# A scan and a gated MLP on one core: new orders for five queues, tiles assigned by a table, and PSUM banks in two sets

## The chip, the cores and the metric

The kernel runs on one core of one Trainium2 chip. The metric is the device time of one execution in microseconds (us), the median of several runs. The kernel before was timed three times: 179.22, 179.46 and 179.83 us. Lower is better.

The engines are named as in the profile: PE multiplies matrices, ACT evaluates functions and copies, DVE works on vectors, POOL does a few small things, SP starts nearly all DMA transfers. Each of them takes its instructions strictly in the order in which they were emitted.

## The reference

For x of shape 2048 x 512 (bfloat16), xn is x with each row normalized. Two branches read xn, and their product is added to x:

```python
xn = _layernorm(x, axis=-1)
Bu = einsum(xn, B_bar)                 # complex, 512 states; B_bar = (exp(dt*Lam)-1)/Lam * B
for t in range(2048): h = Lam_bar * h + Bu[t]
s = 2 * einsum(hseq, C).real + xn * Dskip
g = silu((gelu(xn @ w_gate) * (xn @ w_up)) @ w_down)    # 512 -> 1376 -> 512
out = x + s * g
```

## The kernel before

The 2048 rows are cut into four slabs of 512 (s = 0 to 3), and each slab into four tiles of 128 rows (m = 0 to 3). The steps of a slab are these; the line numbers are those of the profile.

* **Normalizing.** Slab 0 is centred tile by tile as its rows land (`center`, L341 to L350), turned by PE through PSUM (`head_t`, L315, L330, copied by L321, L323, L332 into `xcT`) and scaled only when products leave PSUM. Slabs 1 to 3 are normalized on ACT into the one buffer `xna` (L756); slab 1 takes its sums on DVE (L281), slabs 2 and 3 take theirs on ACT (L751). Each slab's `xna` is then turned by one DMA (`dma_t4`, L362) into `xnT`.
* **Gated products.** For each tile PE multiplies by `w_up` and `w_gate`, in column pieces of 512, 512 and 352 (L384, L402 for slab 0; L434 for the others). ACT takes each piece out of PSUM, plainly or through gelu (L392, L408, L437). DVE multiplies the two (L416, L418, L443, L445) into `at`, and a DMA turns `at` into `atT` (`at_t`, L450).
* **Down products.** Eleven matmuls a tile with `w_down` (`down_pair`, L466), then silu on ACT into `g2` (L469). Gelu and silu lie in different function tables of ACT, so a change from one to the other costs a table load.
* **The scan.** In two halves of 256 states (`half`), PE multiplies xn by B (L529), ACT copies to `U` (L531), DVE rotates (L541, then L549 or L553 into `W`), scans along time (L560, four a half), carries the last state on (L570 to L573) and rotates back (L541, then L549 or L553 into `hst`).
* **The output.** For each tile ACT writes `sk` = xn x Dskip into a PSUM bank (L478), PE adds eight matmuls of `hst` with the scaled C (`y_part`, L482), DVE multiplies by `g2` (L487) and adds x (L492), and a DMA writes the rows (L495). The last tile is done in two halves of 256 columns.

Setting up, DVE builds rotation tables (L621, copied by ACT at L628 and L629) and the scaled C (L724, L727, from `tF` that ACT writes at L722). C is loaded turned by DMA (L720) into the place of the second `hst`.

The order of the work is written out by hand: each call adds a numbered step to a `Plan`, and `ORDER` (L21 to L45) is the list of step numbers in which the steps are emitted. It mixes the queues of all engines; within each engine it fixes the sequence. The planned durations in the calls are not used when the kernel is built. Two of the eight PSUM banks (`ybank`) hold output tiles, and six (`ring`) are handed out in turn by `bank()` in the order of the calls. Buffers of `at`, `gt`, `ub`, `U`, `g2`, `yg`, `ot` and `sk` follow from the tile's number.

In the order before, PE does slab 0's gated products, slab 0's eight scan products (L529), then slab 0's four down products (L466), and only then slab 1's first products. SP starts, after the last weight of the gates: x of slab 1, Dskip's row, B's imaginary part, `xnT` of slab 0, B's real part, `wd`, three `atT`, x of slab 2, the fourth `atT`, `xnT` of slab 1.

Of the kernel before, what the change touches and what calls it, by code (L numbers as in the profile page):

```python
# [44 lines left out]
)  # L45


class Plan:

    def __init__(self):
        self.steps = []
        self.wrote = {}
        self.read = {}

    def add(self, eng, cost, emit, reads=(), writes=(), **planned):
# [9 lines left out]
        self.steps.append((emit, deps - {n}))  # L67
        return n

    def run(self):  # L70
        done = set()
        for i in ORDER:
            emit, deps = self.steps[i]
            assert deps <= done
            emit()
            done.add(i)
        assert len(done) == len(self.steps)
# [3 lines left out]
def kernel(  # L81
# [63 lines left out]
    gt = [sb(f"gt{i}", [P, F]) for i in range(NGT)]  # L145
    ub = [sb(f"ub{i}", [P, F]) for i in range(NGT)]
# [9 lines left out]
    sk = [sb(f"sk{i}", [P, M, D]) for i in range(2)]  # L156
    NG2 = 3
    g2 = [sb(f"g2_{i}", [P, 2, D], FP32) for i in range(NG2)]
# [9 lines left out]
    NR = 6  # L168
    ring = [psum.tile([P, D], FP32, name=f"ring{i}") for i in range(NR)]
    ybank = [psum.tile([P, D], FP32, name=f"ybank{i}") for i in range(2)]  # L170
# [4 lines left out]
    pl = Plan()  # L175
    DV, AC = 0.075, 0.075
# [46 lines left out]
    W1, W2 = CH[0][1], CH[1][1]  # L223
# [54 lines left out]
    def stats(m):  # L278
        r = 250.0 - 20 * m if m < M else 0.0
        order = head if m == 0 else []  # L280
        dve(512, lambda: V.bn_stats(out=st[:, m, :], in_=x_tok[:, m, :]), [("x", m // M, m % M)], [("st", m)], rank=r, after=order)  # L281
# [13 lines left out]
    def dummies(k, i):  # L295
        def f():
            for j in range(k):
                T.matmul(ybank[j][:] if j < 2 else ring[i][:], lhsT=warm[:, 0:P], rhs=warm, start=True, stop=True)  # L298
        pl.add(PE, k * 0.427, f, [], [("bank", i), ("y", 0), ("y", 1)], lag=0.22, not_before=0.6)

    def fill(k, i):
        def f():
            for _ in range(k):
                T.matmul(ring[i][:], lhsT=warm[:, 0:P], rhs=warm, start=True, stop=True)
        pe(k, 512, f, [], [("bank", i)])

    def head_t(m):

        if m == 0:
            for i in range(2):  # L310
                tp = ring[4 + i][:].bitcast(BF16)[:, 0 : D // 2].rearrange("p (k t) -> p k t", t=P)
# [4 lines left out]
                pe(2, P, f, [("xc", 0, i), "ident"], [("bank", 4 + i)])  # L316
            for i in range(2):
                tp = ring[4 + i][:].bitcast(BF16)[:, 0 : D // 2].rearrange("p (k t) -> p k t", t=P)
                dst = xcT[:, 2 * i : 2 * i + 2, 0:P]
                if i == 0:  # L320
                    head.append(dve(256, lambda tp=tp, dst=dst: V.tensor_copy(out=dst, in_=tp), [("bank", 4)], [("xcT", 0, 0)], rate=2.0, rank=500.0, after=head[-1:]))  # L321
                else:
                    acts(256, lambda tp=tp, dst=dst: act(out=dst, in_=tp, func=AF.Copy), [("bank", 5)], [("xcT", 0, 1)], rank=500.0)  # L323
            return
        bank, key = ybank[(m + 1) % 2], ("y", (m + 1) % 2)
        tp = bank[:].bitcast(BF16)[:, 0:D].rearrange("p (k t) -> p k t", t=P)
# [7 lines left out]
    head, sums0 = [], []  # L334

    def center(m):

        x = x_tok[:, m, :]
        if m == 0:
# [3 lines left out]
            dve(c, lambda: V.tensor_scalar(out=yg[0][:, 0:c], in0=x[:, 0:c], scalar1=1.0 / D, scalar2=None, op0=ALU.mult, op1=ALU.add,  # L343
                                           accum_out=ma[:, 0:1]), [("x", 0, 0)], [("yg", 0, 0), ("ma", 0)], base=0.15, rank=400.0, after=early)
            head.append(dve(512, lambda: V.tensor_scalar(out=xn[0], in0=x, scalar1=ma[:, 0:1], scalar2=mb[:, 0:1], op0=ALU.subtract, op1=ALU.subtract),
                            [("x", 0, 0), ("ma", 0), "mb"], [("xc", 0, 0), ("xc", 0, 1)], rate=2.3, rank=400.0, after=head[-1:]))
# [18 lines left out]

    def skip(s, m):
        dve(512, lambda: V.tensor_tensor(out=sk[s % 2][:, m, :], in0=xn[m], in1=Drow[:], op=ALU.mult),
            [("xn", m), "Drow"], [("sk", s % 2, m)], rate=2.0)


    ring_n = [0]

    def bank():
        r = ring_n[0] % NR
        ring_n[0] += 1
# [457 lines left out]
```

## Time and profile before

| | |
|---|---|
| timed runs | 179.22, 179.46, 179.83 us (median 179.46) |
| profiled execution | span 178.6 us from first to last instruction; its own time is not listed apart from the timed runs, which lie 0.6 to 1.2 us above the span |
| PE | busy 173.1 us (97%), 849 matmuls |
| DVE | busy 156.2 us (87%), 252 instructions |
| ACT | busy 125.1 us (70%), 240 instructions, nine of them table loads of 1.28 us |
| DMA | 18.66 MB moved; busy in nearly every slice up to 45 us, then in bursts |
| granted PE clock | 1.000 |

The span counts from the first to the last instruction. A group's row gives its line, engine, operation and tiles, then the busy time in all, the mean of one instruction in ns, and the idle time of the engine just before such an instruction with what ended it. Instructions of one engine overlap a little, so two starts lie closer together than one duration. A matmul row's mean is longer than the step from one matmul to the next, since matmuls are pipelined: four matmuls of 512 columns take 0.86 us in the chain of waits, and four of 352 columns 0.60 us.

### The profile page before, as it was taken

To read this page: it belongs to the slowest core of one execution; us is meant where nothing else is said; L and a number is where in the kernel's file an instruction comes from. 1 tells how busy PE (TensorE), PEld (TensorE's weight loads), DVE (VectorE), ACT (ScalarE), POOL (GpSimd) and SP (SyncE) were. 2 spreads that over 40 slices of the span, in tenths; PEclk is the share of its full clock that TensorE was granted. 3 is DMA by queue.
4 is the path that set the end of the run, shared out by engine and by line. 5 is a ranking of instruction groups with operands and counts; after the bars stand their busy time and mean duration, and the time that the engine had idled before them with its cause. 6 is when DMAs were issued, how large, how long until landed. Compare 5 with 4: busy or idle time off the path is not lost.

```text
span 178.6 us, 2422 instructions
## 1 busy us (share of the span) xinstructions
PE 173.1 (97%) x849; PEld 82.6 (46%) x849; DVE 156.2 (87%) x252; ACT 125.1 (70%) x240; POOL 10.2 (6%) x25
## 2 busy tenths in 40 slices
PE   8999999699999999999999999999999999999992
PEld 2545554244445554444445544444444455454451
DVE  2859997999769986999999979999999899999664
ACT  6879999969899998996619965474353872474510
POOL 2660020000100000000002000000000000000000
PEclk9999999999999999999999999999999999999999
DMA  5999999999700008920500007529300021077012
GB/s 153 266 343 276 151 275 162 215 278 224 141 0 0 0 0 154 179 60 0 110 0 31 4 2 146 111 68 157 79 25 4 0 51 33 29 161 171 0 37 81
DMA packets 47939, 18.66 MB, mean 104 GB/s; under 512 B 40280, under 2 KB 47288, under 8 KB 47928
## 3 DMA queue, kind: packets, MB, share of 16 engines
q1 hardware_dynamic: 47904, 18.52, 49.4%
q8 instruction: 6, 0.10, 0.2%
q14 instruction: 5, 0.04, 0.1%
q10 hardware_dynamic: 24, 0.00, 0.0%
HBM read 6.46 MB, written 2.10 MB: 48 GB/s over the span
## 4 chain that ended last, share of the span: by engine, by line
PE 87%; DMA 5%; DVE 3%; ACT 3%; issue 0%
PE ring L434 31%; PE ring L466 21%; PE ybank L482 15%; PE ring L529 12%; DMA atT<-at 5%; PE ring L384 3%; PE ring L402 1%; ACT gt L408 1%; PE ring L298 1%; DVE st L281 1%; PE ybank L384 1%; ACT at L392 1%; DVE yg L487 1%; DVE at L416 1%; ACT L408 1%; DVE ot L492 1%
## 5 line engine op out<-in xcount | busy, mean ns | idle before, releaser
L434 PEld LDWEIGHTS <-xnT 128*128 128x128 bf16 x288 | 28.2, 98 | 28.4
L466 PE MATMUL ring<-wd,atT 128*128 128x512 bf16 (+1 forms) x176 | 39.2, 379 | 1.5 <-DMA atT<-at 1.5
L434 PE MATMUL ring<-wu,xnT 128*128 128x512 bf16 (+1 forms) x144 | 32.3, 357 | 0.0
L434 PE MATMUL ring<-wg,xnT 128*128 128x512 bf16 (+1 forms) x144 | 32.1, 357 | 0.0
L560 DVE TENSOR_TENSOR_SCAN Fs<-rho,ini,W 128x512 bf16<-128x512 f32 x24 | 29.6, 1271 | 0.1
L529 PE MATMUL ring<-xnT,BT 128*128 128x512 bf16 x128 | 29.3, 379 | 0.0
L482 PE MATMUL ybank<-C,hst 128*128 128x512 bf16 x120 | 27.9, 379 | 0.0
L466 PEld LDWEIGHTS <-atT 128*128 128x128 bf16 (+1 forms) x176 | 17.1, 98 | 22.6 <-DMA atT<-at 1.9
L437 ACT ACTIVATE ub<-ring 128x512 bf16<-128x512 f32 (+1 forms) x36 | 19.1, 557 | 11.2 <-PE ring L434 10.8
L437 ACT ACTIVATE gt<-ring 128x512 bf16<-128x512 f32 (+1 forms) x36 | 19.1, 559 | 7.7 <-PE ring L434 7.6
L531 ACT ACTIVATE U<-ring 128x512 bf16<-128x512 f32 x32 | 18.0, 599 | 4.2 <-PE ring L529 4.1
L541 DVE TENSOR_TENSOR Q<-U,tab 128x4096 bf16<-128x4096 bf16 x8 | 18.3, 2291 | 1.8 <-ACT U L531 1.1
L482 PEld LDWEIGHTS <-hst 128*128 128x128 bf16 x136 | 13.3, 98 | 13.9
L529 PEld LDWEIGHTS <-BT 128*128 128x128 bf16 x128 | 12.5, 98 | 15.0
L469 ACT ACTIVATE g<-ring 128x512 f32<-128x512 f32 x16 | 9.3, 595 | 14.2 <-PE ring L466 14.2
L541 DVE TENSOR_TENSOR Q<-Fs,tab 128x4096 bf16<-128x4096 bf16 x8 | 18.3, 2290 | 0.2
L487 DVE TENSOR_TENSOR yg<-ybank,g 128x512 bf16<-128x512 f32 x15 | 10.2, 687 | 6.6 <-PE ybank L482 6.6
L478 ACT ACTIVATE ybank<-sk 128x512 f32<-128x512 bf16 x15 | 9.1, 609 | 3.8 <-DVE yg L487 3.8
L751 ACT ACTIVATE junk<-x_tok 128x512 bf16<-128x512 bf16 x16 | 10.1, 642 | 1.7 <-DMA x_tok<-in_A_x_dram 1.7
L402 PE MATMUL ring<-wg,W 128*128 128x512 bf16 (+1 forms) x48 | 9.5, 357 | 0.0
L756 ACT ACTIVATE xna<-x_tok,nb,rs 128x512 bf16<-128x512 bf16 x12 | 9.4, 822 | 0.0
L560 DVE TENSOR_TENSOR_SCAN Fs<-rho,W 128x512 bf16<-128x512 f32 x8 | 9.3, 1208 | 0.0
(124 smaller groups left out, 169.8 us busy)
## 6 DMA issues: line engine op xcount, KB each, us to landing
out_dram<-ot SPq DMA_DIRECT2D x15, 128.0 KB, 1.7
x_tok<-in_A_x_dram SPq DMA_DIRECT2D x3, 512.0 KB, 5.1
wg<-in_B_w_gate_dram SPq DMA_DIRECT2D x1, 1376.0 KB
wd<-in_B_w_down_dram SPq DMA_DIRECT2D x1, 1280.0 KB
wu<-in_B_w_up_dram SPq DMA_DIRECT2D x6, 128.0 KB, 2.4
x_tok<-in_A_x_dram SPq DMA_DIRECT2D x4, 128.0 KB, 2.2
wu<-in_B_w_up_dram SPq DMA_DIRECT2D x1, 352.0 KB, 4.6
wu<-in_B_w_up_dram SPq DMA_DIRECT2D x1, 256.0 KB
```

What stands on the lines that cost most here:

```text
L402: T.matmul(ps[:, 0 : b - a], lhsT=xcT[:, k, m * P : (m + 1) * P], rhs=wt[:, k, a:b], start=(k == 0), stop=(k == KT - 1))
L434: T.matmul(ps[:, 0 : b - a], lhsT=xnT[:, s % 2, m, k, :], rhs=wt[:, k, a:b], start=(k == 0), stop=(k == KT - 1))
L437: acts(b - a, lambda: act(out=dst[:, a:b], in_=ps[:, 0 : b - a], func=AF.Copy if up else AF.Gelu_apprx_tanh), [("bank", r)], [key], table= ...
L466: T.matmul(ps[:], lhsT=atT[:fs, k, m * P : (m + 1) * P], rhs=wd[:fs, k, :], start=(k == 0), stop=(k == NFT - 1))
L482: T.matmul(ps, lhsT=hst[s % 2][:, j // NPT, j % NPT, m * P : (m + 1) * P], rhs=C2[:, j // NPT, j % NPT, c0:c1], start=(j == 0 and not seed ...
L487: dve(w, lambda: V.tensor_tensor(out=yg[e][:, c0:c1], in0=ps, in1=g2[gi][:, b, c0:c1], op=ALU.mult), [key, ("g2", gi, b)], [("yg", e, c0)])
L529: T.matmul(ps[:], lhsT=BT[:, ri, k, pt * P : (pt + 1) * P], rhs=xnT[:, s % 2, :, k, :], start=(k == 0), stop=(k == KT - 1))
L531: acts(512, lambda q=q, ri=ri, ps=ps: act(out=U[ui][:, ri, q, :], in_=ps[:], func=AF.Copy), [("bank", r)], [("U", ui, q, ri)])
L541: dve(4096, lambda: V.tensor_tensor(out=Qf, in0=src.unsqueeze(1).to_broadcast(WQ), in1=table, op=ALU.mult), reads, ["Q"], rate=2.0)
L560: pl.add(DVE, 1.12 if s == 0 else 1.185, lambda ri=ri, q=q, pt=pt, first=first: V.tensor_tensor_scan(out=Fs[:, ri, q, :], data0=rho[:, pt ...
L751: acts(512, lambda i=i, fn=fn, sc=sc, m=m: act(out=junk()[:], in_=x_tok[:, s * M + m, :], func=fn, scale=sc, accum_out=sx[:, s, i, m : m + ...
L756: acts(512, lambda m=m: act(out=xn[m], in_=x_tok[:, s * M + m, :], func=AF.Identity, scale=rs[:, s, m : m + 1], bias=nb[:, s, m : m + 1]), ...
```

## The change

What the kernel computes stays the same. Five things are edited:

1. `ORDER` is a new list. On PE, slab 1's gated and scan products come right behind slab 0's scan products, and slab 0's down products come in between them, later. Down, scan, gated and output products of neighbouring slabs are mixed from there on. The last product of slab 0's gates (tile 2, first 512 columns) moves in between slab 0's scan products. On ACT the silu steps are scattered among the gelu steps: the program has 15 table loads instead of 9. On DVE slab 1's sums come ahead of the rotation tables.
2. On SP, the last columns of `w_up` (352 of them, all rows) are loaded as the sixth transfer instead of the twelfth. B's real part comes ahead of its imaginary part. Behind B come x of slab 2, the last rows of `wd`, x of slab 3, `xnT` of slab 1, and then the body of `wd`, C's imaginary part, and the first `atT`.
3. A table `SLOTS` says which buffer each use takes: PSUM banks, `U`, `g2`, `at`, `yg`, `ot`, `sk`, `atT`. `Plan.run` asserts that a buffer's former user is done in the order.
4. The banks are one list of eight: six (`ps`) for products of 512 columns and for output tiles, two (`pp`) for the products of 352 columns and a few early uses. `gt` and `ub` are cut into a buffer for the first 1024 columns and one for the last 352, `sk` into eight tiles and `g2` into six, with as many bytes as before. A block of `atT` is no longer tied to m.
5. The first tile is centred in two halves of 256 columns, the second half first, and the two halves are turned in that order.

The core of the diff (the lists are left out):

```diff
@@ class Plan
+    def group(self, pool):
+        g = self.groups[pool]
+        self.groups[pool] += 1
+        return g, SLOTS[pool][g]
...
     def run(self):
-        done = set()
+        done, owner = set(), {}
         for i in ORDER:
-            emit, deps = self.steps[i]
+            emit, deps, held = self.steps[i]
             assert deps <= done
+            for g in held:
+                slot = g[0], SLOTS[g[0]][g[1]]
+                was = owner.get(slot, g)
+                assert was == g or not self.left[was]
+                owner[slot] = g
+                self.left[g] -= 1
             emit()
...
-    ring = [psum.tile([P, D], FP32, name=f"ring{i}") for i in range(NR)]
-    ybank = [psum.tile([P, D], FP32, name=f"ybank{i}") for i in range(2)]
+    banks = [psum.tile([P, D], FP32, name=f"bank{i}") for i in range(8)]
...
+    def bank(part=False):
+        pool = "pp" if part else "ps"
+        g, i = pl.group(pool)
+        return (pool, g), banks[SIZES["ps"] + i if part else i]
...
@@ center, the first tile
-            head.append(dve(512, lambda: V.tensor_scalar(out=xn[0], in0=x, scalar1=ma[:, 0:1], scalar2=mb[:, 0:1], op0=ALU.subtract, op1=ALU.subtract),
-                            [("x", 0, 0), ("ma", 0), "mb"], [("xc", 0, 0), ("xc", 0, 1)], rate=2.3, rank=400.0, after=head[-1:]))
+            for i in range(2):
+                c0, c1 = i * HD, (i + 1) * HD
+                dve(HD, lambda c0=c0, c1=c1: V.tensor_scalar(out=xn[0][:, c0:c1], in0=x[:, c0:c1], scalar1=ma[:, 0:1], scalar2=mb[:, 0:1],
+                                                             op0=ALU.subtract, op1=ALU.subtract),
+                    [("x", 0, 0), ("ma", 0), "mb"], [("xc", 0, i)], rate=2.3)
...
@@ gate_tile, product
-            r, ps = bank()
+            key, ps = bank(c == 2)
...
@@ at_t
-        j = (s * M + m) % NAT
-        dma(SP, 1.45, 2.4, lambda: nc.sync.dma_start_transpose(out=atT[:, :, m * P : (m + 1) * P], in_=at[j][:]),
-            [("at", j, c) for c in range(3)] + [("atpad", j)], [("atT", m)], rank=30.0, svc=(3, 1.57, 1.5))
+        g, i = at_of(s, m)
+        gT, iT = atTs[s, m] = pl.group("atT")
+        dma(SP, 1.45, 2.4, lambda: nc.sync.dma_start_transpose(out=atT[:, :, iT * P : (iT + 1) * P], in_=at[i][:]),
+            [("at", g, c) for c in range(3)] + [("atpad", i)], [("atT", gT)], rank=30.0, svc=(3, 1.57, 1.5))
```

More of the change, by code (lines that the diff above doesn't have):

```diff
@@ L21 @@
 ORDER = (
[23 rows of a table removed]
-)
[24 rows of a table added]
+)
+SLOTS = {
[4 rows of a table added]
+    ),
+    "pp": (
+        0, 1, 0, 1, 1, 1, 0, 0, 1, 0, 0, 1, 0, 1, 0, 1, 0, 1, 0, 1, 1, 0, 1, 0, 1, 1, 1, 0, 0, 0, 0, 1, 1, 0, 1, 0, 1, 0, 1,
+    ),
+    "U": (
+        0, 1, 0, 2, 0, 1, 0, 2,
+    ),
+    "g2": (
+        5, 0, 1, 4, 3, 0, 4, 2, 2, 0, 1, 5, 3, 1, 4, 5,
+    ),
+    "at": (
+        2, 1, 0, 3, 2, 0, 1, 1, 1, 0, 2, 3, 2, 3, 1, 0,
+    ),
+    "gtA": (
+        0, 0, 1, 1, 0, 1, 0, 1, 1, 0, 0, 0, 1, 1, 0, 0,
+    ),
+    "gtB": (
+        1, 1, 0, 0, 0, 0, 1, 1, 1, 0, 0, 0, 0, 1, 0, 1,
+    ),
+    "ubA": (
+        0, 1, 0, 0, 1, 1, 1, 0, 0, 0, 1, 1,
+    ),
+    "ubB": (
+        0, 0, 1, 1, 1, 0, 0, 1, 0, 0, 1, 0,
+    ),
+    "yg": (
+        0, 0, 1, 1, 0, 1, 0, 1, 0, 1, 1, 0, 0, 0, 1, 0, 1, 0,
+    ),
+    "ot": (
+        1, 1, 1, 0, 1, 0, 0, 0, 0, 0, 0, 1, 1, 0, 1, 0, 1,
+    ),
+    "sk": (
+        2, 3, 0, 1, 5, 7, 4, 6, 0, 1, 3, 2, 5, 4, 6, 7,
+    ),
+    "atT": (
+        0, 1, 3, 0, 1, 1, 3, 2, 0, 3, 2, 1, 1, 2, 3, 0,
+    ),
+}
+SIZES = {"ps": 6, "pp": 2, "U": 3, "g2": 6, "at": 4, "gtA": 2, "gtB": 2, "ubA": 2, "ubB": 2, "yg": 2, "ot": 2, "sk": 8, "atT": 4}
 class Plan:
@@ L279, in stats @@
         r = 250.0 - 20 * m if m < M else 0.0
-        order = head if m == 0 else []
-        dve(512, lambda: V.bn_stats(out=st[:, m, :], in_=x_tok[:, m, :]), [("x", m // M, m % M)], [("st", m)], rank=r, after=order)
+        dve(512, lambda: V.bn_stats(out=st[:, m, :], in_=x_tok[:, m, :]), [("x", m // M, m % M)], [("st", m)], rank=r)
         dve(6, lambda: V.bn_aggr(out=mv[:, m, :], in_=st[:, m, :]), [("st", m)], [("mv", m)], rank=r + 5 if r else 0.0)
@@ L293, in rstd, with dummies @@
              rank=250.0 - 20 * m0)
-    def dummies(k, i):
+    def dummies(k):
+        held = [bank(True), bank(True), bank()]
         def f():
             for j in range(k):
[L298 to L305, printed above, removed]
+                T.matmul(held[min(j, 2)][1][:], lhsT=warm[:, 0:P], rhs=warm, start=True, stop=True)
+        pl.add(PE, k * 0.427, f, [], [b[0] for b in held], lag=0.22, not_before=0.6)
     def head_t(m):
@@ L364, in dma_t4, with at_of @@
             [("xn", m) for m in range(M)], [("xnT", s % 2, m) for m in range(M)], rank=20.0, after=list(sp_last) if s == 0 else (), svc=TURN)
+    sks = {}
     def skip(s, m):
[L367 to L375, printed above, removed]
-        return r, ring[r]
+        g, i = pl.group("sk")
+        sks[s, m] = ("sk", g), sk[i]
+        dve(512, lambda: V.tensor_tensor(out=sk[i][:], in0=xn[m], in1=Drow[:], op=ALU.mult), [("xn", m), "Drow"], [("sk", g)], rate=2.0)
+    opened, ats, gts = {}, {}, {}
+    def at_of(s, m):
+        if (s, m) not in ats:
+            ats[s, m] = pl.group("at")
+        return ats[s, m]
     def up_rows(m, k, c):
         a, b = CH[c]
-        ps, key = (ring[2 * m + c], ("bank", 2 * m + c)) if m < 3 else (ybank[c], ("y", c))
+        if (m, c) not in opened:
+            opened[m, c] = bank(m == 3)
+        key, ps = opened[m, c]
         def f():
@@ L402, in f @@
                 T.matmul(ps[:, 0 : b - a], lhsT=xcT[:, k, m * P : (m + 1) * P], rhs=wt[:, k, a:b], start=(k == 0), stop=(k == KT - 1))
-        pe(KT, b - a, f, [("xcT", m, 0), ("xcT", m, 1)] + [(nm, k, c) for k in range(KT)], [("bank", r)])
+        pe(KT, b - a, f, [("xcT", m, 0), ("xcT", m, 1)] + [(nm, k, c) for k in range(KT)], [key])
         if nm == "wu":
-            out_up(m, c, ps, ("bank", r))
+            out_up(m, c, ps, key)
             return
-        q = m % NGT
-        acts(b - a, lambda: act(out=gt[q][:, a:b], in_=ps[:, 0 : b - a], func=AF.Gelu_apprx_tanh, scale=rs[:, 0, m : m + 1]),
-             [("bank", r), ("rs", 0, m)], [("gt", 2 * q + c) if c < 2 else ("gtb", q)], ptr=1, table="gelu", rank=80.0 - 10 * m)
+        gk, dst, _ = gate_out(0, m, c)
@@ new lines, in first_w, with gated @@
+        acts(b - a, lambda: act(out=dst, in_=ps[:, 0 : b - a], func=AF.Gelu_apprx_tanh, scale=rs[:, 0, m : m + 1]),
+             [key, ("rs", 0, m)], [gk], ptr=1, table="gelu", rank=80.0 - 10 * m)
+    def gated(s, m):
+        g, i = at_of(s, m)
+        for lo, hi in ((0, 2), (2, 3)):
+            a, b = CH[lo][0], CH[hi - 1][1]
+            gk = [gate_out(s, m, c)[0] for c in range(lo, hi)]
+            gtile = gate_out(s, m, lo)[2]
+            if s == 0:
+                uk, utile = [("at", g, "up", c) for c in range(lo, hi)], at[i][:, a:b]
+            else:
+                uk, utile = [up_out(s, m, c)[0] for c in range(lo, hi)], up_out(s, m, lo)[2][:]
+            dve(b - a, lambda a=a, b=b, gtile=gtile, utile=utile: V.tensor_tensor(out=at[i][:, a:b], in0=gtile[:], in1=utile, op=ALU.mult),
+                gk + uk, [("at", g, c) for c in range(lo, hi)], rate=2.0)
@@ L434, in f @@
                     T.matmul(ps[:, 0 : b - a], lhsT=xnT[:, s % 2, m, k, :], rhs=wt[:, k, a:b], start=(k == 0), stop=(k == KT - 1))
-            pe(KT, b - a, f, [("xnT", s % 2, m)] + [(nm, k, c) for k in range(KT)], [("bank", r)])
-            key = ("ub" if up else "gt", 2 * q + c) if c < 2 else ("ubb" if up else "gtb", q)
-            acts(b - a, lambda: act(out=dst[:, a:b], in_=ps[:, 0 : b - a], func=AF.Copy if up else AF.Gelu_apprx_tanh),
-                 [("bank", r)], [key], table=None if up else "gelu")
+            pe(KT, b - a, f, [("xnT", s % 2, m)] + [(nm, k, c) for k in range(KT)], [key])
@@ L453, with f @@
     g2s = {}
-    g2_n = [0]
     def down_pair(s, h):
-        gi = g2_n[0] % NG2
-        g2_n[0] += 1
-        for b in range(2):
-            m = 2 * h + b
-            r, ps = bank()
-            def f(m=m, ps=ps):
+        for m in (2 * h, 2 * h + 1):
+            key, ps = bank()
+            gT, iT = atTs[s, m]
+            def f(iT=iT, ps=ps):
                 for k in range(NFT):
                     fs = min(P, F - k * P)
-                    T.matmul(ps[:], lhsT=atT[:fs, k, m * P : (m + 1) * P], rhs=wd[:fs, k, :], start=(k == 0), stop=(k == NFT - 1))
-            pe(NFT, 512, f, [("atT", m), "wd0", "wd"], [("bank", r)])
-            g2s[s, m] = (gi, b)
-            acts(512, lambda b=b, ps=ps: act(out=g2[gi][:, b, :], in_=ps[:], func=AF.Silu), [("bank", r)], [("g2", gi, b)], table="silu", rank=3.0)
@@ L471, with y_part @@
-    y_n = [0]
-    def y_part(s, m, c0, c1, bank, key, seed, e):
+                    T.matmul(ps[:], lhsT=atT[:fs, k, iT * P : (iT + 1) * P], rhs=wd[:fs, k, :], start=(k == 0), stop=(k == NFT - 1))
+            pe(NFT, 512, f, [("atT", gT), "wd0", "wd"], [key])
+            g, i = g2s[s, m] = pl.group("g2")
+            acts(512, lambda i=i, ps=ps: act(out=g2[i][:], in_=ps[:], func=AF.Silu), [key], [("g2", g)], table="silu", rank=3.0)
+    def y_part(s, m, c0, c1):
         w = c1 - c0
-        ps = bank[:, 0:w]
-        if seed:
-            acts(w, lambda: act(out=ps, in_=sk[s % 2][:, m, c0:c1], func=AF.Copy), [("sk", s % 2, m)], [key])
+        key, bk = bank()
+        ps = bk[:, 0:w]
+        kk, skt = sks[s, m]
+        acts(w, lambda: act(out=ps, in_=skt[:, c0:c1], func=AF.Copy), [kk], [key])
@@ L482, in f @@
                 T.matmul(ps, lhsT=hst[s % 2][:, j // NPT, j % NPT, m * P : (m + 1) * P], rhs=C2[:, j // NPT, j % NPT, c0:c1],
-                         start=(j == 0 and not seed), stop=(j == 2 * NPT - 1), skip_group_check=True)
-        pe(2 * NPT, w, f, [("hst", s % 2, 0), ("hst", s % 2, 1)] + C2S + ([key] if seed else []), [key])
-        gi, b = g2s[s, m]
-        if seed:
-            dve(w, lambda: V.tensor_tensor(out=yg[e][:, c0:c1], in0=ps, in1=g2[gi][:, b, c0:c1], op=ALU.mult), [key, ("g2", gi, b)], [("yg", e, c0)])
-        else:
-            ys = tF[:, 0, c0:c1]
-            dve(w, lambda: V.tensor_tensor(out=ys, in0=ps, in1=sk[s % 2][:, m, c0:c1], op=ALU.add), [key, ("sk", s % 2, m)], [("tF",)])
-            dve(w, lambda: V.tensor_tensor(out=yg[e][:, c0:c1], in0=ys, in1=g2[gi][:, b, c0:c1], op=ALU.mult), [("tF",), ("g2", gi, b)], [("yg", e, c0)])
@@ L492, in y_part @@
-        dve(w, lambda: V.tensor_tensor(out=ot[e][:, c0:c1], in0=yg[e][:, c0:c1], in1=x_tok[:, s * M + m, c0:c1], op=ALU.add),
-            [("yg", e, c0), ("x", s, m)], [("ot", e, c0)], rate=2.0)
+                         start=False, stop=(j == 2 * NPT - 1), skip_group_check=True)
+        pe(2 * NPT, w, f, [("hst", s % 2, 0), ("hst", s % 2, 1)] + C2S + [key], [key])
+        gg, ig = g2s[s, m]
+        gy, iy = pl.group("yg")
+        go, io = pl.group("ot")
+        dve(w, lambda: V.tensor_tensor(out=yg[iy][:, 0:w], in0=ps, in1=g2[ig][:, c0:c1], op=ALU.mult), [key, ("g2", gg)], [("yg", gy)])
@@ L497, in y_tile @@
     def y_tile(s, m):
-        i = y_n[0] % 2
-        seed = True
-        y_n[0] += 1
-        if (s, m) == (NS - 1, M - 1):
-            for h in range(2):
-                r, ps = bank()
-                y_part(s, m, h * HD, (h + 1) * HD, ps, ("bank", r), True, m % 2)
-        else:
-            y_part(s, m, 0, D, ybank[i], ("y", i), seed, m % 2)
-    u_n = [0]
+        cuts = (0, HD, D) if (s, m) == (NS - 1, M - 1) else (0, D)
+        for c0, c1 in zip(cuts, cuts[1:]):
+            y_part(s, m, c0, c1)
@@ L529, in f @@
                         T.matmul(ps[:], lhsT=BT[:, ri, k, pt * P : (pt + 1) * P], rhs=xnT[:, s % 2, :, k, :], start=(k == 0), stop=(k == KT - 1))
-                pe(KT, 512, f, [("BT", ri)] + [("xnT", s % 2, m) for m in range(M)], [("bank", r)])
-                acts(512, lambda q=q, ri=ri, ps=ps: act(out=U[ui][:, ri, q, :], in_=ps[:], func=AF.Copy), [("bank", r)], [("U", ui, q, ri)])
+                pe(KT, 512, f, [("BT", ri)] + [("xnT", s % 2, m) for m in range(M)], [key])
+                acts(512, lambda q=q, ri=ri, ps=ps: act(out=U[ui][:, ri, q, :], in_=ps[:], func=AF.Copy), [key], [("U", ug, q, ri)])
         WQ = [P, 2, 2, H2 * TS]
@@ L581, in parameters @@
     def parameters():
-        pt_ps = ring[3][:].bitcast(BF16)
+        key, ps = bank()
+        pt_ps = ps[:].bitcast(BF16)
         def f():
@@ L586, in f @@
             T.transpose(pt_ps[:, 4:12], pv1[:, :], ident[0:8, 0:8])
-        pe(2, 60, f, [("pv", i) for i in range(3)] + ["ident"], [("bank", 3)])
-        dve(12, lambda: V.tensor_copy(out=pf[:], in_=pt_ps[:, 0:12]), [("bank", 3)], [("pf", 0), ("pf", 1)], rank=245.0)
+        pe(2, 60, f, [("pv", i) for i in range(3)] + ["ident"], [key])
+        dve(12, lambda: V.tensor_copy(out=pf[:], in_=pt_ps[:, 0:12]), [key], [("pf", 0), ("pf", 1)], rank=245.0)
         pool(1.15, lambda: G.tensor_tensor(out=dt_[:], in0=e_t[:], in1=ldt, op=ALU.pow), [("pf", 0), "e_t"], ["dt"], rank=245.0)
```

102 lines of the change are left out of this document (59 added, 43 removed), and 51 rows, old and new, of tables (ORDER, SLOTS).

## The prediction

> **What bounds the kernel now.** I read the page's engine shares first, then the waits, the chain in order of time, the DMA queue's issues, and the timelines of DVE and ACT.
>
> ```profile
> span 178.6 us, 2422 instructions
> PE 173.1 (97%) x849; PEld 82.6 (46%) x849; DVE 156.2 (87%) x252; ACT 125.1 (70%) x240; POOL 10.2 (6%) x25
> ...
> PE ring L466 <- DMA atT<-at: 1.5, 1, 1.5
> PE ybank L298 <- PEq L817: 0.8, 1, 0.8
> ...
> 23.62 9.38 DMA atT<-at
> 33.00 0.05 issue
> 33.05 9.69 PE ring L466 x44
> 42.73 6.05 PE ring L529 x28
> ```
>
> The first two lines show PE nearly always busy. The waits of PE alone are two: the start, and 1.5 us before the first down product. In the chain PE then runs without a hole from 33.05 us to its last matmuls. So what the change can win on PE is that wait and a little of the start; the rest of PE's time is matmuls that stay.
>
> ```profile
> 21.77 0.58 SPq L675 DMA_DIRECT2D wd<-in_B_w_down_dram  x1
> 22.40 1.12 SPq L676 DMA_DIRECT2D wd<-in_B_w_down_dram  x1
> 23.62 9.89 SPq L450 DMA_TRANSPOSE atT<-at  x3
> 33.56 0.57 SPq L216 DMA_DIRECT2D x_tok<-in_A_x_dram  x1
> 34.19 1.42 SPq L450 DMA_TRANSPOSE atT<-at  x1
> 35.71 3.63 SPq L362 DMA_TRANSPOSE xnT<-xna  x1
> ```
>
> SP's queue shows why PE waited: the first turned `at` is started behind 1.4 MB of `wd` and lands at 33.0 us. It also shows `xnT` of slab 1 only at 35.7 us, which the new order needs earlier.
>
> ```profile
> 164.16 2.29 DVE L541 TENSOR_TENSOR Q<-Fs,tab 128x4096 bf16<-128x4096 bf16 x1
> 166.48 1.23 DVE L553 TENSOR_TENSOR hst<-Q 128x2048 bf16<-128x2048 bf16 x1
> ...
> L469 ACT ACT_TABLE_LOAD x4 | 5.1, 1283 | 0.1
> L437 ACT ACT_TABLE_LOAD x3 | 3.8, 1283 | 0.1
> ```
>
> DVE finishes the last `hst` at 167.7 us, and PE starts slab 3's output tiles at 168.2: a room of half a microsecond. DVE is thus the second bound, hidden just behind PE.
>
> **The change, part by part.**
>
> *PE's own work.* From the first scan product of slab 0 (24.52 us before) the same matmuls remain: by the chain's steps 0.216 us for 512 columns (0.863 for four) and 0.149 for 352. That is 128 of L529 (27.6), 176 of L466 (38.0), 120 and 16 half ones of L482 (25.9 and 1.7), 192 and 96 of L434 (41.4 and 14.3), together 149.0. Without any wait PE would end at 24.5 + 149.0 = 173.5 us; the same steps counted on from 33.05 us make it end at 175.1 in the kernel before, and 3.5 us of eviction and output DMA follow up to 178.6. So the wait that goes is worth 1.6 us (1.45 of it the row's), at most.
>
> *The start.* The 512-wide subtraction (0.41 us, L345) becomes two; the nearest rows are its half (0.21) and a 256-wide DVE copy (0.29). The first turned half is ready about 0.15 us sooner, the second no sooner. ACT copies its half right after the second tile's sums, ahead of two squares (0.9 us each), instead of at 5.30 us. I take -0.2 for PE, between -0.6 (PE's first matmuls start when the transposes do) and +1.1: the 352 KB load took 4.6 us to land, so the early columns, started near 3.1 us, are there by 7.7 at worst, and PE asks for them at about 6.6. By bytes, 992 KB at the 254 to 278 GB/s of those microseconds from 2.0 us, they are there by 6.5, so I take no wait. PE then reaches slab 1's first product at 24.5 + 6.9 - 0.2 = 31.2.
>
> *`xnT` of slab 1 at 31.2 us.* This is the wait that can replace the old one. Its rows need slab 1's sums. x of slab 1 lands 9.0 us after its start at 6.93, at 15.9, which is unchanged; DVE now stands waiting for it from about 11.7, where its scaling of slab 0 (L358) ends, as the table steps that filled this time come later. Four L281 and four L282 steps (0.62 and 0.09), three `sk` products (0.34), POOL's L744 and L745 (1.35) and one gate product give `nb` at about 21.0. ACT is behind its gelus until 23.0, then four L756 (steps of 0.70) end at 25.9. SP is free by then: B's two turns and `xnT` of slab 0 end at 21.7 as before, then x of slab 2, 96 KB of `wd`, x of slab 3. Alone, a turn of `xna` took 4.3 us: 30.2. Behind big loads it is slower. The first `atT` landed 5.0 us after the data of `wd` had ended (28.0); 1120 KB behind B's turn (23.7) at 310 GB/s end at 27.3, which gives 32.3. I take 31.6, between the two as the load ahead is smaller: a wait of 0.4, from 0 to 1.1. Everything started behind it on SP, `wd` first, is not needed until the first down product at 48.5.
>
> *ACT.* Evictions are as many as before, plus six table loads at 1.283 (7.7 us); ACT then carries 133 of 178 us. It waits in order, so I added its steps up (0.50 us for a 512-wide one, 0.36 for 352, 0.76 for a sum, 0.70 for L756) and set them against the time at which PE wants each bank. The smallest rooms are -0.1 at 70.3 us, 0.15 at 42.5, 0.05 at 119 and 120; the same sums for the order before have no room under 0.4. I take 0.3 for small waits, from 0 to 1.5. They do not add to the others: a PE that is already late finds its banks free. The new banks take nothing themselves.
>
> The Trainium skill (ScalarE: Activation LUTs, "What ACT_TABLE_LOAD costs") speaks against such a change: a switch costs 1283 ns and a drain of some 1380 besides, and it advises to group functions by table. The rows here show the first part and not the second: an eviction ends at 16.22, the load runs from 16.23 for 1.28, and the next gelu starts at 17.53. By the Trainium skill the six switches are 16.0 us, and ACT carries 141; what that would make of the time is a rival below.
>
> *DVE to the end.* From `nb` of slab 1 to the last `hst` the new order holds 32 scans (38.7 us at steps of 1.21), 16 rotations L541 (2.27, 36.3), 8 and 12 sums L549 and L553 (0.62 and 1.20, 19.4), six table steps (7.2), 15 gate products of each kind (13.5), 11 pairs of L487 and L492 (0.65 and 0.37, 11.3), 8 C steps (5.6), 13 `sk` (4.4) and small ones (4.9): 141.3. From 21.0 that is 162.3 with no wait. Before, the like sum is 131.5 from 28.5, and `hst` was done at 167.7, so 7.7 us were waits: for the outputs' PE (3.3), for C's `tF` (2.9), for `U` and the tables (1.5). The first kind goes, since DVE is now behind PE there. The other two stay in part: DVE meets the second `tF` 1.6 early, and the copied table (L628, which moved to the end of that stretch on ACT) 0.7 early. I take 2.3 of waits, from 0.5 to 5: `hst` at 164.6. Behind it in the queue stand the last gate products (down product of tile 3 at 169) and the banks of two output tiles.
>
> *The sum.* The last `hst` reaches PE at 164.8; after it come three output tiles (5.2), the last down product (2.4) and the last output tile (1.7): PE ends at 174.1, where fed without a wait it would end at 173.3. The two waits above (0.4, 0.3) lie inside this 0.8. Against 175.1 that is 1.0 us less, and the end behind PE is the same: two halves, 3.5 us. Span 178.6 - 1.0 = 177.6. The profiled execution's span lies 0.9 us under the median of the timed runs (0.6 to 1.2 under the three), so the time is 179.46 - 1.0 = 178.5.
>
> **The rivals.** A difference of 0.3%, about 0.54 us, is what a measurement of this kernel can tell from none.
>
> *Nothing binds.* Waits on DVE shrink below 1.5 us and `xnT` lands by 31.2: PE ends at 173.3, 1.8 us earlier than before, which is 177.7 us. For it: PE ran 142 us without a hole before. Against it: the rooms are thinner now.
>
> *DVE becomes the bound (slower).* DVE idles about 4 us at 11.7 that it filled with table steps before. With w of waits, PE ends at 162.3 + 0.2 + w + 9.3. From w = 3.3 on it is no faster, from 3.8 on it is slower; with 5.5 it is 181.7, and with the former 7.7, 183.9. For it: 7.7 before, and 87% busy. Against it: 3.3 of these were waits for PE's output tiles.
>
> *`xnT` of slab 1 late (slower).* If the two slab loads ahead of it hold its issue as `wd` held `atT` (5.7 us in the queue) and its rows come 2 us later, it lands at 34.3; DVE and ACT follow PE, so 178.5 + 2.3 = 180.8. It decides from 33.6 on, where PE is 2.4 us late.
>
> *Table switches.* A switch stops ACT for twice the load's row, since the engine empties first: between 71 and 78 us ACT has two switches ahead of a bank with 0.3 of room, so PE is 2 x 1.28 - 0.3 = 2.3 late there, 1.5 later than I have it: 180.0. No row of before shows such a stop. This is the rule of the Trainium skill named above.
>
> *The reorder does nothing.* One wait for another of the same 1.5 us, with the start unchanged: 179.4.
>
> **How the numbers follow.** My forecast (178.0 to 178.9) 0.40, nothing binds 0.13, no change 0.16, DVE 0.17, late `xnT` 0.09, switches 0.05. Faster by over 0.3%: 0.40 and 0.13, and a little from no change's edge, 0.54; the three slower ones less the part of DVE's case that ends near zero, 0.28; same 0.18. The range leaves out the far ends of the slower cases and of a start that gains 0.6: 177.3 to 180.7. My own case's range is 178.0 to 178.9.
>
> **What would show it.** Right: the 1.5 us wait of L466 is gone; a wait of PE for `xnT`, under 1.1 us, stands near 31 us in its place; the last `hst` ends near 164.6 and PE's first output tile of slab 3 follows at once; 15 table loads of 1.28; PE's last matmul near 174. Wrong: holes of PE of over a microsecond between 40 and 160 us, the granted clock below 1.0, or a last `hst` after 166.

## The result: 0.5% faster, with no wait of PE behind the start

The changed kernel takes 179.0 us (178.64 to 179.5, 22 runs), the kernel before beside it on the same chip 179.75 (179.15 to 181.4, 22 runs). The ratio is 0.9951, with a 95% interval from 0.9935 to 0.9967. A second comparison, on another occasion, gave 179.13 against 180.13: 0.9947 (0.9927 to 0.9968). By the ratio that is 0.9 us less (0.75 between the medians), where the forecast was 1.0 less; the time itself was forecast at 178.5, 0.5 too low.

The head of the page of the changed kernel:

```profile
span 177.3 us, 2419 instructions
...
PE 172.1 (97%) x834; PEld 82.3 (46%) x849; DVE 154.4 (87%) x253; ACT 133.0 (75%) x246; POOL 10.7 (6%) x25
```

The waits of PE, all of them:

```profile
PE bank L374 <- PEq L903: 0.8, 1, 0.8
PE bank L461 <- DMA wu<-in_B_w_up_dram: 0.4, 1, 0.4
```

The wait for the first `atT` is gone and none for `xnT` has come in its place. The second line is new: at 10.9 us PE waits 0.4 us for the last rows of `w_up`. SP's queue shows why `xnT` (L435) comes in time; the columns are start, duration and the instruction:

```profile
21.78 0.58 SPq L291 DMA_DIRECT2D x_tok<-in_A_x_dram  x1
22.41 0.50 SPq L762 DMA_DIRECT2D wd<-in_B_w_down_dram  x1
22.96 0.42 SPq L291 DMA_DIRECT2D x_tok<-in_A_x_dram  x1
26.19 2.74 SPq L435 DMA_TRANSPOSE xnT<-xna  x1
28.98 0.58 SPq L761 DMA_DIRECT2D wd<-in_B_w_down_dram  x1
```

The turn is started at 26.19 and the trace gives 4.2 us from its issue to its landing: 30.4. PE asks for it at 31.7. The timelines of DVE and PE at the end, in the changed kernel:

```profile
159.16 2.29 DVE L626 TENSOR_TENSOR Q<-Fs,tab 128x4096 bf16<-128x4096 bf16 x1
161.38 0.69 DVE L517 TENSOR_TENSOR at<-gtA,ubA 128x1024 bf16<-128x1024 bf16 x1
161.98 1.22 DVE L638 TENSOR_TENSOR hst<-Q 128x2048 bf16<-128x2048 bf16 x1
```

```profile
159.84 4.92 PE L563 MATMUL bank<-wd,atT 128*128 128x512 bf16 x21
164.59 5.34 PE L578 MATMUL bank<-C,hst 128*128 128x512 bf16 x24
169.78 2.54 PE L563 MATMUL bank<-wd,atT 128*128 128x512 bf16 x11
172.15 1.91 PE L578 MATMUL bank<-C,hst 128*128 128x256 bf16 x16
```

DVE has the last `hst` ready at 163.2, and PE takes it up at 164.6 without waiting. PE's last matmul ends at 174.06, and 3.2 us of eviction and output follow. The forecast of 174.1 for this end was counted in steps; by the same steps the kernel before ended at 175.1, and by its timeline at 175.41. So between these two executions PE's end moved by 1.35 us, not by the 1.0 that was forecast. The terms behind it were others too, as the experiments show.

### The profile page after: what moved, and what is told of

It is laid out like the page before. It is cut to its first block, busy times and chain, and to the rows that moved or that the text cites. A ratio compares the mean times of both kernels' runs of the same rounds, so it can differ in the third digit from the quotient of the medians.

```text
span 177.3 us, 2419 instructions
## 1 busy us (share of the span) xinstructions
PE 172.1 (97%) x834; PEld 82.3 (46%) x849; DVE 154.4 (87%) x253; ACT 133.0 (75%) x246; POOL 10.7 (6%) x25
## 4 chain that ended last, share of the span: by engine, by line
PE 91%; DMA 4%; SPq 1%; issue 1%; DVE 0%
PE bank L535 31%; PE bank L563 21%; PE bank L614 16%; PE bank L578 16%; PE bank L498 6%; DMA wu<-in_B_w_up_dram 3%; PE bank L461 2%; DMA x_tok<-in_A_x_dram 1%; SPq L287 1%; SPq L296 0%; DVE yg L584 0%; DVE ot L585 0%
## 5 line engine op out<-in xcount | busy, mean ns | idle before, releaser
L563 PE MATMUL bank<-wd,atT 128*128 128x512 bf16 (+1 forms) x174 | 40.2, 379 | 0.1
L535 PE MATMUL bank<-wu,xnT 128*128 128x512 bf16 (+1 forms) x140 | 31.9, 356 | 0.1
L535 PE MATMUL bank<-wg,xnT 128*128 128x512 bf16 (+1 forms) x139 | 31.7, 356 | 0.3
L614 PE MATMUL bank<-xnT,BT 128*128 128x512 bf16 x128 | 30.9, 379 | 0.1
L578 PE MATMUL bank<-C,hst 128*128 128x512 bf16 (+1 forms) x134 | 29.7, 366 | 0.1
L538 ACT ACTIVATE ubA<-bank 128x512 bf16<-128x512 f32 x24 | 14.6, 614 | 8.7 <-PE bank L535 8.3
L616 ACT ACTIVATE U<-bank 128x512 bf16<-128x512 f32 x32 | 19.0, 618 | 1.7 <-PE bank L614 1.7
L538 ACT ACTIVATE gtA<-bank 128x512 bf16<-128x512 f32 x24 | 14.8, 616 | 5.3 <-PE bank L535 4.6
L584 DVE TENSOR_TENSOR yg<-bank,g 128x512 bf16<-128x512 f32 (+1 forms) x17 | 11.1, 654 | 5.1 <-PE bank L578 4.9
L498 PE MATMUL bank<-wg,W 128*128 128x512 bf16 (+1 forms) x47 | 9.7, 356 | 0.1
```

What stands on the lines that cost most here:

```text
L498: T.matmul(ps[:, 0 : b - a], lhsT=xcT[:, k, m * P : (m + 1) * P], rhs=wt[:, k, a:b], start=(k == 0), stop=(k == KT - 1))
L535: T.matmul(ps[:, 0 : b - a], lhsT=xnT[:, s % 2, m, k, :], rhs=wt[:, k, a:b], start=(k == 0), stop=(k == KT - 1))
L538: acts(b - a, lambda: act(out=dst, in_=ps[:, 0 : b - a], func=AF.Copy if up else AF.Gelu_apprx_tanh), [key], [ok], table=None if up else " ...
L563: T.matmul(ps[:], lhsT=atT[:fs, k, iT * P : (iT + 1) * P], rhs=wd[:fs, k, :], start=(k == 0), stop=(k == NFT - 1))
L578: T.matmul(ps, lhsT=hst[s % 2][:, j // NPT, j % NPT, m * P : (m + 1) * P], rhs=C2[:, j // NPT, j % NPT, c0:c1], start=False, stop=(j == 2 ...
L584: dve(w, lambda: V.tensor_tensor(out=yg[iy][:, 0:w], in0=ps, in1=g2[ig][:, c0:c1], op=ALU.mult), [key, ("g2", gg)], [("yg", gy)])
```

## The experiments

A table holds what the runs have in common. S is the start of the first scan product of slab 0, E the end of PE's last matmul, both from PE's timeline; the wait is what the view of waits gives for PE in between. In the changed kernel one gate product of 0.86 us lies behind S that lies ahead of it in the kernel before.

| profiled execution | S | E | E - S | wait of PE in between |
|---|---|---|---|---|
| before (178.6 us) | 24.52 | 175.41 | 150.89 | 1.5, `atT` |
| before, second (177.5) | 24.91 | 174.26 | 149.35 | none |
| before, third (177.5) | 24.49 | 174.30 | 149.81 | 0.4, `atT` |
| before, one turn moved | 24.71 | 173.97 | 149.26 | none |
| changed (177.3) | 23.95 | 174.06 | 150.11 | none |
| changed, again (177.4) | 24.07 | 174.18 | 150.11 | none |
| changed, rows later | 23.48 | 173.59 | 150.11 | none |
| changed, one table | 23.73 | 173.85 | 150.12 | none |
| changed, DVE +1.2 | 23.56 | 173.67 | 150.11 | none |
| changed, DVE +2.4 | 23.84 | 174.73 | 150.89 | 0.6, `hst` |
| changed, turn behind `wd` | 23.86 | 178.26 | 154.40 | 2.4, `xnT` |
| changed, turn behind nine tenths | 24.03 | 177.08 | 153.05 | 2.8, `xnT` |

Five executions of the changed order without a wait agree to 0.01 us from S on: 150.11, or 149.25 without that gate product. Nothing but the matmuls themselves sets this stretch.

### Does the new load order cost the 0.4 us at 10.9?

```diff
 ORDER = (
-    ..., 87, 102, 98, 85, 111, 103, 96, 59, 82, 58, 63, 116, 172, 88, 168, 157, 90, 104, 86, ...
+    ..., 87, 85, 82, 86, 102, 98, 111, 103, 96, 59, 58, 63, 116, 172, 88, 168, 157, 90, 104, ...
```

> The changed kernel, with three of PE's k=2 products (0.65 us) moved ahead of the first product that reads the last rows of w_up. Theory A (the new load order makes PE wait 0.38 us at 10.87 us for these rows, and nothing behind it binds): the wait is gone, the first scan product comes at 23.7 instead of 24.11, PE's last matmul 0.3 to 0.4 earlier, 178.6 us against 179.0. Theory B (the last hst of DVE sets the end): the start moves by 0.4, PE then waits as much for hst near 164, and the time stays at 179.0. Theory C (xnT of slab 1 is late once PE comes earlier): PE waits up to 0.4 us near 32, 179.0.

Measured: 179.14 us, ratio 0.9972 (0.9947 to 0.9997). The wait is not there in its profile and S is 23.48, but the time is that of the changed kernel (one of the twelve runs took 181.04; no trace shows why). Theory A falls as a statement on the time. B and C fall as well: PE has no wait for `hst` or `xnT`. The run with one function table and the one with DVE's sum made twice, both below, show why the time does not fall: they keep the changed kernel's start and have no such wait either (S at 23.73 and 23.56). The 0.4 us belonged to that one execution.

### The kernel before, with one turn started earlier

```diff
 ORDER = (
-    ..., 150, 151, 175, ...
+    ..., 175, 150, 151, ...
```

150 and 151 are the two loads of `wd`, 175 the turn of the first `at` that PE asks for.

> The kernel before, with the turn of the first gate tile started ahead of the two wd loads in SP's queue instead of behind them; nothing else is moved. The first atT should land near 26 us instead of 33.0 and PE's wait of 1.5 us shrink to between 0 and 0.9 (the second turn now stands behind wd). Theory A (the wait alone was to be won, on PE): 178.3 to 179.2 us against 179.75. Theory B (DVE's last hst, which came 0.5 us ahead of PE, was as good as the bound): at most 0.5 us less, 179.25, and a wait of PE for hst of up to 1 us near 167.

Measured: 178.98 us against 179.93, ratio 0.9945 (0.9925 to 0.9964): as much as the whole change. The times also lie closer together, as they should where a wait that varies is gone: seven runs from 178.59 to 179.26, where the 27 of the kernel before beside them go from 179.23 to 180.72. SP's queue and PE's timeline of this kernel (its lines are one further than before):

```profile
21.80 1.59 SPq L451 DMA_TRANSPOSE atT<-at  x1
23.43 0.82 SPq L676 DMA_DIRECT2D wd<-in_B_w_down_dram  x1
24.30 0.67 SPq L677 DMA_DIRECT2D wd<-in_B_w_down_dram  x1
26.45 4.85 SPq L451 DMA_TRANSPOSE atT<-at  x2
```

```profile
24.71 7.07 PE L530 MATMUL ring<-xnT,BT 128*128 128x512 bf16 x32
31.62 4.70 PE L467 MATMUL ring<-wd,atT 128*128 128x512 bf16 x20
```

Ahead of `wd` the turn takes 1.6 us in the queue instead of being held there, and the down products follow the scan products without a gap. Theory A holds. Theory B does not: the last `hst` came earlier too, at 166.3 instead of 167.7, 0.6 us ahead of PE at 166.9, as it was 0.6 ahead before (167.7 and 168.3). DVE's queue shows the reason. Its last wait for PE ahead of that `hst` is for an output tile; first in the kernel before, then here:

```profile
142.54 1.29 DVE L487 TENSOR_TENSOR yg<-ybank,g 128x512 bf16<-128x512 f32 x2 [0.69 <-PE ybank L482]
141.10 1.29 DVE L488 TENSOR_TENSOR yg<-ybank,g 128x512 bf16<-128x512 f32 x2 [0.68 <-PE ybank L483]
```

When PE comes 1.4 us earlier, so does this step, and all that stands behind it in DVE's queue. The two further executions of the kernel before, below, have the same wait (0.69) and the same lead of `hst` (0.6). DVE's wait for `tF` fell as well, from 2.9 to 1.3, but it lies ahead of this one. So what had looked like a second bound close behind PE was DVE following PE.

### One function table

```diff
-func=AF.Gelu_apprx_tanh
+func=AF.Silu
```

> The changed kernel with silu in the place of gelu (another function of the same length: the output is not the reference's), so that ACT's 14 further table loads, 18 us, are gone. Theory A (the loads lie in rooms of ACT): 179.0, within 0.3. Theory B (the six added loads stop ACT on the path, by twice the row of 1.28 in two places): 1.5 us less, 177.5. In between, the small waits of ACT that I took at 0.3: 178.7.

Measured: 179.08 us, ratio 0.9952 (0.9935 to 0.9969). ACT's busy time fell from 133.0 to 115.1 us, one table load is left, and the time did not move. Theory A holds. In the changed kernel ACT's timeline shows what a switch is:

```profile
61.77 0.47 ACT L538 ACTIVATE gtB<-bank 128x352 bf16<-128x352 f32 x1
62.25 1.28 ACT L566 ACT_TABLE_LOAD   x1
63.55 1.09 ACT L566 ACTIVATE g<-bank 128x512 f32<-128x512 f32 x2
```

An eviction ends at 62.24, the load runs from 62.25 to 63.53, the next function starts at 63.55. The Trainium skill (ScalarE: Activation LUTs, "What ACT_TABLE_LOAD costs") adds a drain of some 1380 ns to the load; here ACT stands idle for 0.03 us around the load, so the trace disagrees, and the measurement decides.

### How much room DVE has

```diff
-                dve(2048, lambda: V.tensor_tensor(out=dst, in0=Qf[:, 0, :, :], in1=Qf[:, 1, ::-1, :], op=ALU.add), ["Q"], writes, rate=2.0)
+                def total():
+                    for _ in range(2 if (s, h, back) == (NS - 1, 1, False) else 1):
+                        V.tensor_tensor(out=dst, in0=Qf[:, 0, :, :], in1=Qf[:, 1, ::-1, :], op=ALU.add)
+                dve(2048, total, ["Q"], writes, rate=2.0)
```

> The changed kernel with DVE's last sum into hst (2048 wide, 1.23 us) made twice. Theory A (DVE is ready 1.4 us ahead of PE there): 0 to 0.2 us more, PE still without a wait for hst. Theory B (DVE's last hst sets the end): 1.2 us more, 180.2.

Measured: 178.94 us, ratio 0.9956 (0.9938 to 0.9973), PE without a wait. Theory A holds. With range(3) in the place of range(2):

> The changed kernel with DVE's last sum into hst made three times (2.44 us more). With one repeat hst was ready 0.25 us ahead of PE. Theory A (a room of 1.4 to 1.5 us, then DVE sets the end): PE waits 0.9 to 1.1 us for hst near 164.4, and the time is 1.0 us more, 180.0. Theory B (PE or DVE fills the hole with other work): under 0.4 us more.

Measured: 179.74 us, 0.6 above the changed kernel's 179.13 in the same comparison; ratio to the kernel before 0.9986 (0.9965 to 1.0006). The waits of PE:

```profile
PE bank L374 <- PEq L907: 0.8, 1, 0.8
PE bank L578 <- DVE hst L641: 0.6, 1, 0.6
```

DVE now sets the end, as A said, but by 0.6 us instead of 1.0 (and 150.89 instead of 150.11 in the table): PE had two matmuls of the output tile to do before it needed the last half. The two repeats added 2.44 us, of which 0.6 to 0.8 were seen at PE's end; DVE's room in the changed kernel is thus 1.7 to 1.8 us.

### Was the wait in the kernel before always the same?

Two more profiled executions of the unchanged kernel. The second:

> The kernel before, unchanged, in another profiled execution. The one that the prediction read had a span of 178.6 us, where the median span of 27 timed executions is 178.1. Theory A (the landing of the first atT varies from one execution to the next, and with it the wait): a span near 178.1 and a wait of PE for atT of 0.9 to 1.2 us instead of 1.45. Theory B (the wait is the same in each execution): 1.4 to 1.5 us again.

The third, after the second had shown a span of 177.5 us and no wait:

> The kernel before, unchanged, in a third profiled execution (one of 178.6 us had a wait of PE for atT of 1.45 us, one of 177.5 none). Theory A (the wait differs by execution, by the landing of the turn, and carries the difference of the spans): span less 177.5 is the wait within 0.3 us, whatever the span. Theory B (the start or the end make the difference): no such relation.

Their times were 179.26 and 179.33 us.

PE's timeline of the third execution has the wait in brackets:

```profile
24.49 7.07 PE L529 MATMUL ring<-xnT,BT 128*128 128x512 bf16 x32
31.94 9.69 PE L466 MATMUL ring<-wd,atT 128*128 128x512 bf16 x44 [0.38 <-DMA atT<-at]
```

The second execution has no wait at all, the third 0.4, the one that the prediction read 1.5; in SP's queue the three turns of `at` took 8.69, 8.82 and 9.89 us, in this order. So the wait differs by execution, and A's first number (0.9 to 1.2) was as wrong as B's. The relation that I expected of the third (span less 177.5) misses by 0.4, because the starts differ as well: S is 24.91 without a wait and 24.49 with 0.4. What holds for the three executions, within 0.1, is that E is S plus the wait plus 149.4. The timed spans of the kernel before have a median of 178.3 in the second comparison (23 runs, 177.4 to 179.5), those of the changed kernel 177.35 (12 runs, 176.6 to 177.6). If the starts and the ends are alike on average, a usual wait is about 0.9 us; that is worked out and not seen in a trace.

### The changed kernel again

> The changed kernel, unchanged, beside the others on this chip. Theory A (PE's wait of 0.4 us for w_up at 10.87 us was that execution's, as two later runs with the same start did not have it): a wait of 0 to 0.2, the first scan product between 23.7 and 24.0; time 179.0, as the kernel before with the one turn ahead (178.98). Theory B (the wait belongs to the new load order): 0.3 to 0.5 again.

```profile
PE bank L374 <- PEq L903: 0.8, 1, 0.8
PE bank L498 <- DMA wu<-in_B_w_up_dram: 0.3, 1, 0.3
PE bank L399 <- DVE xna L423: 0.2, 1, 0.2
```

Neither theory fits whole. The wait at 10.9 is gone, as A said, but one of 0.3 us stands at 7.4, in front of the early columns (L498), and S is 24.07, where A had 23.7 to 24.0. The run with DVE's sum made three times has it too (0.4); the second and third execution of the kernel before wait 0.2 and 0.3 for `w_up` at about 5. In S, counted to the same matmul by adding 0.86, the seven executions with the changed kernel's own start give 24.4 to 24.9, with a mean of 24.72; the four with the start before 24.5 to 24.9, with a mean of 24.66. The new start neither wins nor loses what these can show.

### What a late `xnT` would have cost

```diff
 SP's queue
-    x of slab 2, wd (last rows), x of slab 3, xnT of slab 1, wd (body), C, ...
+    x of slab 2, wd (last rows), x of slab 3, wd (body), xnT of slab 1, C, ...
```

> The changed kernel with slab 1's xnT turn started behind the 1280 KB load of wd in SP's queue instead of ahead of it. Theory A (a turn waits for the plain loads ahead of it, and PE has nothing else ready): xnT lands between 33.5 and 36 us, PE waits 1.5 to 3.5 us near 32.4, and the whole wait stays in the time: 180.5 to 182.5. Theory B (the queues share, the turn is not held up): it lands near 32.5, the time stays at 179.0.

Measured: 182.94 us, ratio 1.0174 (1.0121 to 1.0226). The turn lands 8.1 us after its issue, at 34.2, and PE waits 2.4 us: A's mechanism, but the time is 0.4 above A's range, since E - S is 4.3 us longer and not 2.4:

```profile
34.22 1.76 PE L614 MATMUL bank<-xnT,BT 128*128 128x512 bf16 x4 [2.43 <-DMA xnT<-xna]
```

The windows of 32 to 34, 34 to 37 and 37 to 40 us, with the busy time and count of PE, PEld, DVE, ACT, POOL, then the granted clock, the DMA share and GB/s:

```profile
32.00:34.00 2.00, 0.00 (x0) 0.00 (x0) 2.00 (x3) 1.37 (x5) 0.00 (x0) 1.00 1.13 256
34.00:37.00 3.00, 2.78 (x9) 1.23 (x10) 3.00 (x11) 0.98 (x2) 0.00 (x0) 0.56 1.22 228
37.00:40.00 3.00, 3.00 (x14) 1.26 (x13) 3.00 (x14) 1.66 (x5) 0.00 (x0) 0.87 1.08 213
```

After the stop the granted clock is 0.56 on average for 3 us, and 0.50 in the two single microseconds from 35 to 37. From the end of the wait to the same scan product further on PE takes 7.80 us (34.22 to 42.02); in the next run, whose clock stays whole, 6.12. These 1.7 us are nearly all that the wait leaves of the 4.3.

A last run, to find how long a stop must be for this:

```diff
 SP's queue, against the run above
-    wd (last rows), x of slab 3, wd (ten tenths of the body), xnT of slab 1
+    x of slab 3, wd (last rows), wd (nine tenths of the body), xnT of slab 1, wd (one tenth)
```

> The changed kernel with nine tenths of wd (1152 KB and the 96 KB) loaded ahead of slab 1's xnT turn, and one tenth behind it, where the last run had all of it ahead, waited 2.4 us at xnT and then had half the granted clock for 3 us. By the bytes (128 KB at about 310 GB/s) the turn lands 0.4 us earlier, near 33.8, and PE waits 1.7 to 2.2 us. Theory A (the clock falls only after a stop of more than 2 us; a stop of 1.45 left it whole): the time is 2 us more than that of the changed kernel, 181.1, clock 1.0 after the wait. Theory B (any stop of 1.7 us or more costs the clock): 182.6, with a granted clock near 0.5 for some 3 us.

Measured: 182.16 us (180.9 to 183.53, 4 runs), ratio 1.0136 (1.0059 to 1.0212). The turn did not land earlier: 34.7 us, 8.4 after its issue, and PE stood for 2.8 us. PE's wait and the same windows of this run:

```profile
34.72 1.04 PE L614 MATMUL bank<-xnT,BT 128*128 128x512 bf16 x4 [2.76 <-DMA xnT<-xna]
32.00:34.00 2.00, 0.00 (x0) 0.00 (x0) 2.00 (x2) 1.55 (x5) 0.00 (x0) 1.00 0.90 204
34.00:37.00 3.00, 2.28 (x12) 1.19 (x13) 3.00 (x8) 1.08 (x2) 0.00 (x0) 1.00 0.96 169
37.00:40.00 3.00, 3.00 (x17) 1.47 (x15) 3.00 (x18) 2.47 (x6) 0.00 (x0) 1.00 1.15 225
```

The longer stop left the clock at 1.00, and E - S is longer by 2.9, hardly more than the wait. So both theories fall: the length of the stop does not decide it by itself. The timed runs say the same. With all of `wd` ahead of the turn two of four have a mean clock of 0.99 (spans of 181.5 and 182.3), the others 1.00 (180.7 and 180.8); with nine tenths one of four has 0.99 (181.7), the others 1.00 (179.1 to 180.5).

## Why the prediction came out right

The time was forecast at 178.5, 1.0 less than before; it is 0.9 less, and at 179.0 it lies 0.1 above the range of my own case (178.0 to 178.9). The sign and the chain of causes up to the wait were right: the wait of PE for the first `atT` was what could be won. That the size fits is in part luck. The wait was priced at 1.6 us where the usual one is near 0.9, and 0.8 of it was taken off again for DVE, which bound nothing; these two errors nearly cancelled. Two of the signs that were named did not appear: no wait for `xnT` near 31 us, and the last `hst` came 1.4 us ahead of PE instead of just ahead of it.

* **PE's own work**: right. 149.0 us were summed up from the first scan product on; the table gives 149.25 for the changed kernel and 149.3 to 149.4 for the one before.
* **The wait that goes, worth 1.6 us at most**: right for the execution that was read, too large for the usual one. The step that failed is the base: I set the profiled execution's span against the median of the times and took the 0.9 us between them for what lies around a span. In the timed runs each time lies 1.79 us above its own span, so the profiled execution, with its 178.6, was 0.3 to 0.5 us slower than the median spans of 178.1 (27 runs) and 178.3 (23 runs). The other two profiles have waits of 0.4 and 0. The usual wait is nearer to 0.9. From the right base, 178.6 + 1.79 = 180.4, the same sum would have given 179.4.
* **The start, -0.2**: mis-sized; it is 0.06 by the means above, with 0.5 from one execution to the next. The halves did not bring the first product forward: in the trace DVE does the second tile's subtraction (0.35 us, L423) ahead of the copy of the first turned half, which thus starts at 4.64 instead of 4.36. "I take no wait" for the early columns is wrong in some executions by 0.3 to 0.4 us.
* **`xnT` of slab 1**: the term of 0.4 was 0. `nb` came at 21.7 (21.0 forecast), the turn was started at 26.2 (25.9), and landed at 30.4, by the lower end of the 30.2 to 32.3 that I had. The two slab loads ahead of it did not hold it up as 1280 KB of `wd` did in the last two runs.
* **ACT**: no PE wait for a bank behind the start, where I took 0.3. The count of 133 us was right, and 18 of them can be taken away without a change.
* **DVE to the end, `hst` at 164.6**: this failed by its size. From `nb` to the last `hst` the window from 21.9 to 163.2 holds 137.0 us of DVE's work in 141.3; I had summed 141.3 of work, by chance the length of this window, and added 2.3 of waits. The sum took its steps a little too long: for example a rotation at 2.27, where the next instruction starts 2.20 to 2.22 us behind it, a scan at 1.21, where four take 4.56 to 4.81. The waits were 3.3 (`sk` 1.5, `tF` 0.8, the table 0.6, `at` 0.4), more than I took, yet `hst` was done at 163.2. With the 1.7 to 1.8 us of room that the repeats found, DVE bound nothing; I had it take 0.8 us of the gain. The reading behind it, that DVE is a second bound just behind PE, was wrong already for the kernel before, where DVE waits for PE at 142.5.
* **The rivals**: "nothing binds" is what happened behind the start, but its 177.7 was 1.3 too low, 0.9 of it by the same base. "DVE becomes the bound" needed w = 3.8 on top of too large a sum of work. "Late `xnT`" is a real mechanism of this kernel, priced too low: 2.4 us of wait cost 4.3 where the clock fell with it. "Table switches" is out, by the run with one table. "The reorder does nothing" is out for the kernel as it is; but the one turn moved ahead of `wd`, with the old order, gives the same time.

So the new PE order is one way to be elsewhere when the first `atT` lands. What gave the time was that PE no longer depends on that landing; the tables of buffers, the bank sets, the halves and the early columns are not seen in it. By the timelines the last `hst` is ready 1.4 us ahead of PE, and 0.6 in the old order, where DVE follows PE; how much room DVE has in the old order was not measured. No kernel here beat both: the two fixes meet at the same limit, PE's matmuls from 4 us on.

## What to carry to other kernels

A wait at a DMA's landing can differ from one execution to the next (0, 0.4 and 1.5 us here): before it is priced from one profile, set that profile's span against the spans of the timed runs. When a single transfer is late, look at what stands ahead of it in its queue first; moving one turn ahead of two large loads did what a new order of five queues did. A second engine that finishes just ahead of the first may be there because it follows it, so look for its own waits for the first, and repeat its last step to see its room.

## What was not expected of the hardware

* A stop of PE of 2.4 us was followed by a granted clock of 0.50 to 0.69 for about 3 us; one of 2.8 us in nearly the same place was not, nor was that of 1.5 us in the kernel before. The Trainium skill (TensorE: Matmul & The Clock Gate, Part 1) says that the clock falls to half after an idle window of some 3.4 us, and that the window runs freely and does not start anew with the kernel. That it differs between like stops agrees with a free window; that 2.4 us were enough does not agree with the length.
* The landing of a turn behind plain loads did not follow the bytes ahead of it. Behind two slabs of x and 96 KB it landed 4.2 us after its issue; with 1280 KB more ahead 8.1, and with 1152 KB more 8.4, though 128 KB less had to be moved first. The turns of `at` in the unchanged kernel differ by 1.2 us from one execution to the next.
